# A gated recurrence and a three-way maxout layer on one core: another order of the same pieces

## The chip, the cores and the metric

The kernel runs on one core of a Trainium2 chip. A core has five instruction streams that run side by side and meet by semaphores: TensorE (PE, matrix products, with its weight loads as PEld), VectorE (DVE), ScalarE (ACT), GpSimd (POOL) and SyncE (SP), which here only issues DMAs. ScalarE can issue DMAs too. The metric is the device time of one execution in microseconds (us); lower is better.

## The reference

Four batches of 8 heads, 768 time steps and a head width of 48. For each head a 48x48 state decays row by row and takes in an outer product at every step:

```
state = alpha[:, :, t, :, None] * state + einsum('bhd,bhe->bhde', k[:, :, t], v[:, :, t])
y[:, :, t] = einsum('bhd,bhde->bhe', q[:, :, t], state)
```

The outputs of all heads, side by side (3072 tokens x 384), go through a layer with three weight matrices and a maximum, and an output matrix:

```
h = np.maximum(np.maximum(x @ w1, x @ w2), x @ w3)      # 384 -> 768
out = h @ w_out                                          # 768 -> 384, float32
```

## The kernel before

The 3072 tokens are cut into 12 steps of 256 tokens; steps 0 to 3 are the first 256 tokens of the four batches, 4 to 7 the second, 8 to 11 the third. Within a step the recurrence is done in two chunks of 128 tokens: the cumulated decays are sums of logarithms, a product with a triangular matrix gives them for all tokens, keys and queries are scaled by the exponentials, a masked product of scaled queries and keys gives the part of a chunk within itself, and the state that is carried from chunk to chunk gives the rest.

All work of all steps is cut into pieces, each a small function of step, index and engine. One string, ORDER, lists the pieces; `emit` goes through it from left to right and issues each. `h1v@3` reads: piece h, index 1, on VectorE (v; a is ScalarE, p GpSimd, nothing is the piece's default), step 3. Each engine gets its instructions in the order of the string, and a piece starts when those before it on its engine and what it reads are done. So nothing is planned while the kernel runs: the string is the plan. The pieces:

- `l` loads 256 tokens (384 KB) of alpha, key, query or value (index 0 to 3) into a ring of four buffers, so the load of step s waits for the last reader of step s-4. `K` loads one of 12 parts (384 KB) of the weights into one of 8 staging buffers, `W` casts it to 16 bits (L104 to L111, L174 on). Without a letter, the load is issued by SyncE; with `a`, by ScalarE (L85 to L97).
- `m`, `N`, `r`: products of neighbouring decays, their logarithms, inverses. `u`, `w`: keys and queries of the even tokens scaled by their neighbour's decay. `c`: the sums of the logarithms on TensorE (L207, L209). `e`, `f`, `g`: exponentials of them. `k`, `q`: the scalings of keys and queries (L231). `V`, `v`: scaled values, and their copies by chunk.
- `T`, `t`: turn scaled keys and queries on TensorE, copy them out of PSUM (L265, L151); `D`: turn them by a DMA that SyncE issues (L273). Steps 0 to 4 use `T`, steps 5 to 11 `D`.
- `A`, `a`: scores on TensorE (L286), masks on VectorE (L293). `Y`: outputs on TensorE (L306); even indices are the part within a chunk, odd ones the state's. `x` copies them out as the input x of the layer.
- `M`, `S`, `s`, `z`, `y`: the state: products of gates, update on TensorE (L357), sum (L367), decay (L372), copies in 16 bits.
- `G`: a gate, 6 products of 256 columns (L388), nine for each step; `h`: for every third gate a plain eviction from PSUM (L149 on ScalarE or L151 on VectorE), for the others a maximum on VectorE (L405).
- `O`, `o`: the output projection, 6 products of 384 columns (L421), and its scaling (L155 on ScalarE, L157 on VectorE) with the store that SyncE issues (L430).
- `H`: idle products: so many 128x512 products on a block of zeros, into a PSUM bank that nobody reads (L435).

Everything that TensorE writes goes into eight PSUM banks that are handed out in turn; a piece that needs one waits until the reader of an earlier one is done. Each `H` takes one bank, however many products it has. There are 8 semaphores for DMAs, so a DMA also waits for the eighth before it.

Of the kernel before, what the change touches and what calls it, by code (L numbers as in the profile page):

```python
# [23 lines left out]
def kernel(  # L24
# [422 lines left out]
    def emit(order):  # L447
# [11 lines left out]
        Y3@0 l0@3 v1a@1 t0v@1 m0v@3 A1@1 A0@1 x0a@0 x1a@0 G1@0 K2@0 W2p@0 G2@0 l1@2 a2@1 v0a@1  # L459
        y0p@1 Y3@1 k1p@2 u0p@2 a1@1 N0@3 c0@3 a3@1 a0@1 Y0@1 r0@2 r1@2 K0@0 W0a@0 x0v@1 Y2@1  # L460
        x1a@1 l2@2 s1v@0 s1v@1 f0@3 k0p@2 w0v@2 G0@0 l3@2 M0p@2 G1@1 G0@1 G2@1 h0a@0 q1v@2 T1@2
        g0@3 K5@0 K3@0 e0@3 h1v@0 V0a@2 S0@2 s0a@2 h0v@1 q0p@2 h1v@1 T0@2 t0a@2 t1v@2 W5p@0 G5@1
        G5@0 W3a@0 z0p@2 y0a@2 s1v@2 l0@4 v1p@2 h2v@0 K4@0 h2v@1 r0@4 A1@2 A0@2 a0@2 G3@1 h3a@1
        Y3@2 m0p@4 W4p@0 l3a@3 a3@2 G3@0 N0@4 a1@2 v0p@2 l1@3 r0@3 G4@1 c0@4 g0@4 a2@2 Y2@2
        x1v@2 h3a@0 Y0@2 x0a@2 u0p@3 h4v@1 l0@5 G4@0 h5v@1 M1p@0 z1p@0 y1a@0 G0@2 h0a@2 G5@2
        r1@3 G1@2 K6@0 W6a@0 G3@2 h4v@0 h5v@0 h1v@2 G2@2 l2@3 k0p@3 w0v@3 q0v@3 K7@0 G6@2 V0a@3
        h3a@2 l2@4 l1@4 r1@4 m0p@5 M0p@3 h2v@2 G4@2 h4v@2 k1p@3 S0@3 s0v@3 N0@5 G6@1 h6a@2 h5v@2
        W7p@0 r0@5 G7@2 h7v@2 T0@3 q1p@3 T1@3 G7@1 z0p@3 K8@0 e0@4 w0p@4 f0@4 l3@4 s1v@3 v0a@3
        t1v@3 t0a@3 k1v@4 G6@0 h6a@1 q1p@4 h7v@1 l2@6 u0p@4 c0@5 A0@3 a0@3 A1@3 T1@4 q0p@4 a2@3
        W8a@0 G8@2 a3@3 h8v@2 G8@0 g0@5 h6a@0 a1@3 f0@5 G8@1 k0p@4 T0@4 e0@5 h8v@1 G7@0 v1p@3  # L470
        Y0@3 Y2@3 t1a@4 V0a@4 t0a@4 h7v@0 y0p@3 Y3@3 x0a@3 x1a@3 K11@0 l1@5 K9a@0 v1p@4 S0@4
        W11a@0 A0@4 s0v@4 K10a@0 a1@4 A1@4 a3@4 M0p@4 z0p@4 s1v@4 u0p@5 G0@3 l0@6 a0@4 G7@3
        l1a@6 a2@4 v0v@4 y0a@4 m0p@6 r0@6 G3@3 h3a@3 G1@3 G6@3 Y0@4 r1@5 l3a@5 h0v@3 Y3@4 h8v@0
        Y2@4 x1v@4 N0@6 Y1@4 x0a@4 W9a@0 l2@5 G8@3 M1v@1 c0@6 e0@6 f0@6 G0@4 h1v@3 k0v@5 q1v@5
        G3@4 w0v@5 q0v@5 M0p@5 W10a@0 g0@6 u0v@6 r1@6 G1@4 l0@7 m0v@7 G2@4 k1p@5 D1@5 h0a@4
        z1p@1 k0p@6 O0@1 h1v@4 w0v@6 D0@5 q0p@6 D0@6 k1p@6 q1p@6 O1@1 N0@7 l0@8 h6a@3 l3@6 h2v@4
        l2@7 l1a@7 o1a@1 h7v@3 D1@6 h3v@4 o0a@1 V0a@5 O0@2 o0a@2 O1@2 y1p@1 G7@4 h8v@3 S0@5 A0@5
# [66 lines left out]
```

## Time and profile before

| | us |
|---|---|
| runs | 149.18, 152.22, 148.98 (median 149.18) |
| span of the profiled execution, first to last instruction | 147.1 |
| runs' median over that span | 2.1 |
| TensorE busy | 137.7 |
| VectorE busy | 120.5 |
| ScalarE busy | 100.7 |
| GpSimd busy | 89.7 |
| first sums / first gate / last product's end | 6.18 / 19.22 / 143.2 |

The page gives no time of its own for the profiled execution beside its span; what lies around the span is therefore taken from the runs. Busy times of TensorE are modelled ends of pipelined products, so that the starts of runs of equal instructions say more on their price than the mean of one. DMA issues and waits don't count as busy.

### The profile page before, as it was taken

The page shows a single profiled execution, that of the slowest core. Times are in us where ns is not written, and L with a number is a line of the kernel's source. Part 1 is how long each engine was busy: PE and PEld are TensorE (multiplying, and loading weights), DVE is VectorE, ACT ScalarE, POOL GpSimd, SP SyncE. Part 2 cuts the span into 40 slices and gives each one's busy share as a digit, 9 for nine tenths or more (in the row PEclk, how much of TensorE's full clock was granted, in tenths as well). Part 3 has the DMA queues.
Part 4 walks back from the last instruction along what each step waited for, and adds up shares of the span by engine and source line. Part 5 has one row for each costly group of instructions (what it writes and reads, how often), then busy time and mean ns, then how long its engine had stood idle before and what let it go on. Part 6 is the DMA issues. An engine that isn't in the chain of part 4 may idle for free.

```text
span 147.1 us, 5524 instructions
## 1 busy us (share of the span) xinstructions
PE 137.7 (94%) x2301; PEld 105.4 (72%) x2301; DVE 120.5 (82%) x224; ACT 100.7 (68%) x207; POOL 89.7 (61%) x147
## 2 busy tenths in 40 slices
PE   6996888999999999999999999999899999999990
PEld 2444567888878886788868877688766788878650
DVE  5378989989999999999959998996979989376610
ACT  3669998878999978958699467795375463213170
POOL 8554999899799926997717959738579800000000
PEclk9999999999999999999999999999999999999999
DMA  5999999999999978999999979999987880021163
GB/s 114 321 325 341 326 312 282 322 288 334 328 298 241 286 225 155 202 289 187 303 156 325 327 218 155 237 269 276 288 117 222 91 113 0 4 75 37 53 241 134
DMA packets 73032, 32.43 MB, mean 220 GB/s; under 512 B 65456, under 2 KB 73008, under 8 KB 73008
## 3 DMA queue, kind: packets, MB, share of 16 engines
q1 hardware_dynamic: 63856, 28.06, 75.8%
q10 hardware_dynamic: 9152, 4.03, 10.5%
q8 instruction: 18, 0.29, 0.8%
q14 instruction: 6, 0.05, 0.1%
HBM read 23.69 MB, written 4.72 MB: 193 GB/s over the span
## 4 chain that ended last, share of the span: by engine, by line
PE 38%; DMA 18%; POOL 16%; ACT 9%; SPq 8%; issue 4%; DVE 4%; POOLq 0%; DVEq 0%; ACTq 0%
PE gps L388 21%; DMA rv<-in_v_dram 11%; PE ops L421 10%; SPq L96 7%; POOL qk L231 6%; DMA ws<-in_moe_w_dram 5%; PE yps L306 3%; DMA qkT<-qk 3%; POOL kept L372 2%; POOL ka L198 2%; PE aps L286 2%; POOL st L151 2%; ACT vu L149 1%; POOL wcat L151 1%; POOL vu L151 1%
## 5 line engine op out<-in xcount | busy, mean ns | idle before, releaser
L388 PE MATMUL gps<-xT,wcat 128*128 128x256 f16 x648 | 76.5, 273 | 1.5 <-DVE hT L405 0.6
L388 PEld LDWEIGHTS <-wcat 128*128 128x128 f16 x648 | 61.2, 98 | 11.7 <-issue 1.1
L293 DVE TENSOR_TENSOR lat<-aps,cp 128x512 f16<-128x512 f32 x48 | 30.3, 681 | 0.5 <-PE aps L286 0.3
L405 DVE TENSOR_TENSOR h<-gps,h 128x512 f16<-128x512 f32 x36 | 24.6, 684 | 2.4 <-PE gps L388 1.2
L405 DVE TENSOR_TENSOR hT<-gps,h 128x512 f16<-128x512 f32 x36 | 24.1, 684 | 1.9 <-PE ops L421 1.3
L421 PE MATMUL ops<-wo,hT 128*128 128x384 f16 (+1 forms) x150 | 25.2, 320 | 0.2 <-ACT h L149 0.2
L149 ACT CAST h<-gps 128x512 f16<-128x512 f32 x28 | 16.2, 583 | 9.0 <-PE gps L388 7.0
L421 PEld LDWEIGHTS <-hT 128*128 128x128 f16 x150 | 14.1, 98 | 8.2 <-issue 0.4
L155 ACT ACTIVATE ob<-ops,c 128x384 f32<-128x384 f32 (+1 forms) x23 | 12.2, 567 | 11.4 <-PE ops L421 11.3
L372 POOL TENSOR_TENSOR kept<-full,gm 128x192 f32<-128x192 f32 x18 | 10.3, 573 | 10.5 <-DVE gm L344 5.0
L151 POOL COPY vu<-vt 64x384 f16<-64x384 f16 x24 | 12.2, 509 | 4.7 <-ACT vt L155 2.8
L149 ACT CAST xT<-yps 128x384 f16<-128x384 f32 x17 | 7.8, 490 | 7.3 <-PE yps L306 7.3
L231 POOL TENSOR_TENSOR qk<-ka,ic 128x384 f16<-128x384 f32 x10 | 10.5, 1054 | 3.6 <-ACT h L149 2.6
L149 ACT COPY vu<-vt 64x384 f16<-64x384 f16 x22 | 11.2, 510 | 0.7 <-DVE vt L157 0.3
L435 PE MATMUL wps<-wo 128*128 128x512 f16 x35 | 9.7, 425 | 1.2 <-DVE wo L511 1.2
L155 ACT ACTIVATE vt<-rv,c 128x768 f16<-128x768 f32 x10 | 9.4, 941 | 1.6 <-DMA rv<-in_v_dram 1.5
L231 POOL TENSOR_TENSOR qk<-rq,ac 128x384 f16<-128x384 f32 x8 | 8.3, 1036 | 1.7 <-DMA rq<-in_q_dram 1.7
L286 PE MATMUL aps<-qkT 48*64 48x128 f16 x384 | 7.7, 219 | 1.3 <-DVE qkT L151 0.8
L198 POOL TENSOR_TENSOR ka<-rk,ra 128x384 f32<-128x384 f32 x8 | 8.4, 1044 | 0.2
L306 PE MATMUL yps<-lat,vu 128*32 128x128 f16 x384 | 8.0, 220 | 0.3 <-DVE lat L293 0.2
L231 POOL TENSOR_TENSOR qk<-rk,ic 128x384 f16<-128x384 f32 x6 | 6.2, 1040 | 3.1 <-DMA rk<-in_k_dram 3.0
L192 ACT ACTIVATE ra<-ra 128x384 f32<-128x384 f32 x12 | 6.3, 524 | 2.5 <-DMA ra<-in_alpha_dram 2.4
(58 smaller groups left out, 192.2 us busy)
## 6 DMA issues: line engine op xcount, KB each, us to landing
ra<-in_alpha_dram SPq DMA_DIRECT2D x12, 384.0 KB, 4.9
out_dram<-ob SPq DMA_DIRECT2D x23, 192.0 KB, 2.2
rq<-in_q_dram SPq DMA_DIRECT2D x11, 384.0 KB, 5.9
rv<-in_v_dram SPq DMA_DIRECT2D x9, 384.0 KB, 5.4
ws<-in_moe_w_dram SPq DMA_DIRECT2D x9, 384.0 KB, 5.9
rk<-in_k_dram SPq DMA_DIRECT2D x8, 384.0 KB, 6.1
rk<-in_k_dram ACTq DMA_DIRECT2D x4, 384.0 KB, 5.5
rv<-in_v_dram ACTq DMA_DIRECT2D x3, 384.0 KB, 5.1
```

Source lines behind the costliest of these rows:

```text
L149: nc.scalar.copy(out=dst, in_=src)
L151: engines[eng].tensor_copy(out=dst, in_=src)
L155: nc.scalar.mul(dst, src, col)
L198: engines[eng or "p"].tensor_mul(near_of[s, "k"], raw("k", s, 0), raw("a", s, 1))
L231: engines[eng or "p"].tensor_mul(dst.rearrange("p a b c -> p (a b) c")[:, :, :D], near_of.pop((s, n)) if r == 0 else raw(n, s, r), dec_of[ ...
L286: nc.tensor.matmul(aps[i][r * J:(r + 1) * J, a * U + x, :], qkT[rows, r, 1, p, cols], qkT[rows, :, 0, p, cols], start=True, stop=True)
L293: nc.vector.tensor_mul(lat_of[s, u][:, i], aps_of[s, u][i], pmask.unsqueeze(1).broadcast_to([P, HP, P]))
L306: nc.tensor.matmul(y_of[s, x][C * m:C * (m + 1), f, :], lhs, rhs, start=(s, x, m) not in begun, stop=last[x] and n == len(todo) - 1)
L372: engines[eng or "p"].tensor_mul(kept, full_of.pop((s, x)), gm_of.pop((s, x)).unsqueeze(2).broadcast_to([P, HP, D]))
L388: nc.tensor.matmul(gps[:, j, :], wcat[:, f, g, jj * P:(jj + 1) * P], xT[:, f].rearrange("p u t -> p (u t)"), start=(f == 0), stop=(f == NF ...
L405: nc.vector.tensor_max(h, gps, h_of[s, i - 1])
L421: nc.tensor.matmul(ops_of[s, o], hT_of[s][:, jj, u * P:(u + 1) * P], wo16[:, jj, cols], start=(jj == 0), stop=(jj == NJ - 1))
```

## The change

ORDER is another string. The pieces are the same ones, each as often as before, and the functions are not touched. What differs:

- the place of nearly every piece;
- the engine of some: 8 store scalings, 4 plain evictions, 4 key scalings, 4 gate products and 2 state products move to VectorE, two pieces of the value scaling to GpSimd, and a few single ones either way;
- the issuer of loads: 10 of the 60 were ScalarE's (8 `l` and 2 `K`); all are SyncE's now, and only the two small constants ahead of the string stay ScalarE's;
- the idle products: H12, H4, H1, H1, H4, H10, H1, H2 before, 35 pieces H1 after, 11 of them ahead of the first `c`.

The beginning, the places around the last loads, and the end, cut:

```
-        l0@0 r0@0 H12@0 H4@0 H1@0 m0p@0 N0@0 c0@0 r1@0 l0@1 m0v@1 l2@0 H1@0 r0@1 f0@0 g0@0 H4@0
-        w0p@0 l1@0 u0v@0 q0v@0 N0@1 c0@1 e0@0 l3@0 V0a@0 r1@1 e0@1 f0@1 l0@2 k1v@0 q1v@0 M0p@0
-        l2@1 k0p@0 l1@1 k1p@1 m0v@2 w0v@1 H10@0 g0@1 N0@2 S0@0 s0a@0 T1@0 t1a@0 c0@2 q1v@1 T0@0
-        z0p@0 f0@2 e0@2 g0@2 q0v@1 H1@0 l3@1 V0a@1 t0v@0 A1@0 A0@0 T1@1 H2@0 u0v@1 a2@0 k0p@1
-        S0@1 T0@1 K1@0 v1a@0 v0p@0 a1@0 a3@0 a0@0 Y0@0 W1a@0 Y2@0 t1v@1 y0p@0 s0a@1 M0p@1 z0p@1
...
-        h4v@3 k1v@7 G3@5 h3a@5 G1@5 h1v@5 c0@8 e0@8 g0@7 f0@8 M1p@3 G5@3 h5v@3 G4@5 Y1@6 A1@6
...
-        O4@11 h8v@11 o1a@9 O6@11 o0a@6 o1a@6 o2a@11 O2@11 O3@11 o0a@11 O5@11 o1a@11 O0@10 o0a@10
+        l0@0 m0v@0 l0@1 l2@0 l1@0 m0p@1 l3@0 l2@1 l0@2 N0@0 H1@0 H1@0 H1@0 H1@0 H1@0 H1@0 H1@0 r0@0 H1@0
+        H1@0 H1@0 H1@0 c0@0 H1@0 r0@1 H1@0 H1@0 H1@0 f0@0 r1@0 q1v@0 w0v@0 r1@1 N0@1 e0@0 g0@0 q0v@0 u0v@0
+        k1v@0 H1@0 H1@0 H1@0 H1@0 c0@1 k0v@0 V0v@0 g0@1 f0@1 w0v@1 q1v@1 e0@1 H1@0 H1@0 H1@0 T1@0 H1@0
+        H1@0 S0@0 q0v@1 l1@1 H1@0 T0@0 H1@0 t0v@0 s0v@0 m0p@2 M0p@0 M0v@1 z0p@0 u0v@1 k0v@1 l3@1 t1a@0
+        v1a@0 r0@2 l1@2 K2@0 K0@0 N0@2 r1@2 K1@0 l2@2 l3@2 k1p@1 y0p@0 v0p@0 H1@0 H1@0 H1@0 H1@0 c0@2 A1@0
+        A0@0 T0@1 H1@0 f0@2 s1v@0 a1@0 l0@3 a2@0 a3@0 a0@0 g0@2 V0a@1 t0a@1 S0@1 T1@1 s0a@1 e0@2 W2a@0
...
+        m0p@10 Y0@6 x1a@6 k0v@8 h7v@5 h2v@5 x0a@6 v0a@7 S0@7 s0v@7 A0@7 v0a@8 N0@10 y1a@4 S0@8 A1@7 s0v@8
+        a0@7 G8@5 G5@5 G0@6 a2@7 O1@3 h4v@5 a3@7 o1a@3 G3@6 G1@6 M1v@5 z0v@8 h8v@5 z0p@7 q0p@8 z1p@5 M0p@9
+        q1p@8 y1a@3 y0a@7 h3v@6 a1@7 D0@8 D1@8 l2@11 l3@9 G5@6 G4@6 Y3@7 Y0@7 Y2@7 m0p@11 u0p@9 k1p@9
...
+        G2@6 G7@7 G7@6 c0@11 f0@10 g0@11 f0@11 e0@10 r1@10 y0p@8 w0p@9 q0p@9 V0p@9 k0p@10 k1p@10 v1p@8
...
+        h7v@11 h8v@11 h5v@11 O1@10 o1a@10 o0v@6 O0@10 O4@11 O5@11 O6@11 O2@11 O3@11 o0v@10 o2a@11 o1v@11
+        o0a@11
```

More of the change, by code (lines that the diff above doesn't have):

```diff
@@ L460 @@
[L460 to L477, printed above, removed]
@@ new lines @@
+        Y3@0 H1@0 Y2@0 x1a@0 Y0@0 H1@0 K4@0 z0p@1 x0a@0 K5@0 y0p@1 W1p@0 K3@0 l1@3 t1v@1 k1v@2 u0v@2 W0a@0
+        v0a@1 A0@1 A1@1 a2@1 a0@1 a3@1 H1@0 H1@0 G2@0 G0@0 G1@0 Y3@1 a1@1 Y0@1 v1a@1 V0a@2 s1v@1 w0v@2
+        Y2@1 k0p@2 q1p@2 T1@2 S0@2 x1v@1 x0a@1 h0a@0 G0@1 q0p@2 l0@4 l2@3 s0a@2 h0a@1 T0@2 t0a@2 M0p@2
+        v0p@2 W4p@0 t1v@2 h1v@0 G1@1 G2@1 h2v@0 m0v@3 h1v@1 A1@2 A0@2 N0@3 a2@2 v1a@2 z0p@2 W5p@0 a0@2
+        a1@2 a3@2 c0@3 y0a@2 G4@0 G4@1 G5@0 Y3@2 K6@0 l2@4 l3@3 l1@4 K7@0 e0@3 r0@3 W3p@0 Y2@2 l0@5 Y0@2
@@ new lines @@
+        h2v@1 s1v@2 G3@0 G3@1 k1v@3 x1a@2 r0@4 x0a@2 r1@3 h3v@0 u0p@3 h3v@1 h4v@0 h4v@1 m0p@4 k0p@3 w0p@3
+        r1@4 N0@4 f0@3 G5@1 G0@2 G3@2 c0@4 q1v@3 q0p@3 w0p@4 W6a@0 h3v@2 h5v@0 h5v@1 h0a@2 e0@4 g0@3 G4@2
+        f0@4 T1@3 G1@2 G2@2 T0@3 t1a@3 V0a@3 g0@4 t0a@3 G5@2 G6@0 K10@0 K8@0 l0@6 l3@4 K9@0 K11@0 l1@7
+        l2@5 h1v@2 h4v@2 h2v@2 l0@7 G6@2 S0@3 k1v@4 h5v@2 A0@3 A1@3 h6a@0 W7a@0 s0a@3 G7@0 G7@2 m0v@5 a1@3
+        a0@3 a3@3 q1p@4 u0p@4 M0p@3 v1p@3 M1p@0 q0p@4 N0@5 h6a@2 v0a@3 k0p@4 W8a@0 G6@1 c0@5 T1@4 T0@4
@@ new lines @@
+        h7v@0 a2@3 h7v@2 m0p@6 z0p@3 z1p@0 y0p@3 t1v@4 G8@0 G8@2 W10p@0 r0@5 g0@5 f0@5 N0@6 V0a@4 h8v@0
+        s1v@3 t0v@4 h8v@2 h6a@1 e0@5 G7@1 G8@1 Y2@3 Y0@3 Y3@3 h7v@1 x0a@3 r1@5 x1v@3 S0@4 A1@4 A0@4 s0v@4
+        v0p@4 M1p@1 M0v@4 z1p@1 z0p@4 a2@4 l1@5 a3@4 a0@4 q1v@5 h8v@1 s1v@4 m0v@7 a1@4 u0v@5 v1p@4 u0p@7
+        l1@6 l2@7 l2@6 l3@5 l3@6 l0@9 w0v@5 k0v@5 W9a@0 W11a@0 c0@6 G0@3 G6@3 O0@2 O1@2 O1@1 G4@3 G3@3
+        y1a@0 y0a@4 r0@7 h6a@3 f0@6 e0@6 r1@7 h0a@3 r0@6 g0@6 Y3@4 Y0@4 Y1@4 Y2@4 q0v@5 x0v@4 k1v@5 D0@5
@@ new lines @@
+        D1@5 G7@3 G1@3 M0v@5 l0@8 y1p@1 u0p@6 x1a@4 N0@7 o1a@2 r1@6 h7v@3 o0a@2 k1v@6 w0v@6 h1v@3 G0@4
+        G8@3 c0@7 G1@4 h0v@4 h8v@3 V0a@5 e0@7 o1a@1 O0@1 G2@4 G3@4 G6@4 g0@7 h1v@4 h2v@4 h3v@4 o0a@1 h3a@3
+        f0@7 h4v@3 q0p@6 k0p@6 w0p@7 m0p@9 M0p@6 S0@5 A1@5 A0@5 s0v@5 a3@5 a1@5 a0@5 N0@9 h6a@4 v1a@5
+        v0a@5 M1p@3 q1p@6 M0p@7 z0p@5 G2@3 c0@9 G5@3 O0@0 G7@4 G8@4 y0p@5 M1p@2 m0p@8 h5v@3 a2@5 h2v@3
+        h7v@4 h8v@4 k1v@7 s1v@5 Y2@5 Y3@5 Y1@5 Y0@5 G4@4 D0@6 l1@8 D1@6 g0@9 f0@9 V0a@6 N0@8 x1a@5 x0a@5
@@ new lines @@
+        a2@8 a0@8 D1@9 a1@8 D0@9 a3@8 l3@11 l2@10 G3@7 O0@5 G8@7 G4@7 G2@7 h8v@7 h1v@7 h2v@7 Y0@8 Y3@8
+        Y1@8 Y2@8 o0a@5 v1a@9 h3a@7 x0a@8 x1a@8 g0@10 S0@9 A1@9 A0@9 r0@11 s0v@9 h4v@7 a3@9 a2@9 a1@9 G5@7
+        G3@8 O0@4 G6@8 O1@4 h3v@8 h6a@8 r1@11 V0v@11 z0p@9 w0p@10 y1p@5 q1p@10 o1v@4 h5v@7 q0v@10 q1p@11
+        a0@9 v1p@10 M0p@10 v0p@9 G4@8 h4v@8 G0@8 G7@8 D1@10 D0@10 O0@7 o0a@7 G1@8 G8@8 O1@7 G5@8 y0p@9
+        h7v@8 M1v@6 w0v@11 q0v@11 o0v@4 h8v@8 h0a@8 o1a@7 Y0@9 Y2@9 Y3@9 x1a@9 Y1@9 z1v@6 x0v@9 S0@10
@@ new lines @@
+        A0@10 A1@10 h5v@8 a2@10 G2@8 G7@9 s0v@10 G6@9 a0@10 h1v@8 h6a@9 G3@9 G8@9 G1@9 h2v@8 a3@10 h7v@9
+        u0p@11 M0p@11 k1p@11 h8v@9 G0@9 O1@8 G2@9 y1a@6 h3a@9 v0a@10 v0p@11 z0p@10 k0p@11 y0p@10 a1@10
+        D1@11 O0@8 D0@11 h0v@9 h1v@9 M1v@7 o1v@8 Y2@10 Y1@10 Y0@10 Y3@10 x0a@10 A0@11 h2v@9 x1v@10 S0@11
+        A1@11 O1@6 G0@10 a3@11 a0@11 z1v@7 o0v@8 s0v@11 h0a@10 o1v@6 G6@10 G2@10 G1@10 G4@9 G7@10 h1v@10
+        h4v@9 a2@11 a1@11 G5@9 h5v@9 z0p@11 y0p@11 v1p@11 y1p@7 G8@10 Y1@11 Y0@11 Y2@11 Y3@11 G4@10 G5@10
@@ L507 @@
+        x1a@11 h6a@10 h2v@10 x0v@11 G4@11 G3@10 h3v@10 h4v@10 G0@11 G7@11 h5v@10 G3@11 h3v@11 h7v@10
+        h0a@11 G1@11 O0@9 O1@9 G2@11 o0a@9 O0@6 G6@11 h8v@10 h1v@11 G8@11 G5@11 h6a@11 o1a@9 h2v@11 h4v@11
+        h7v@11 h8v@11 h5v@11 O1@10 o1a@10 o0v@6 O0@10 O4@11 O5@11 O6@11 O2@11 O3@11 o0v@10 o2a@11 o1v@11
+        o0a@11
     """
```

34 lines of the change are left out of this document (6 added, 28 removed).

## The prediction

> **What bounds the kernel now.** I read the page's first part, then the busy times by stretch, the timeline of TensorE and VectorE over the head, the groups, the waits, and the chain that ended last.
>
> ```profile
> span 147.1 us, 5524 instructions
> PE 137.7 (94%) x2301; PEld 105.4 (72%) x2301; DVE 120.5 (82%) x224; ACT 100.7 (68%) x207; POOL 89.7 (61%) x147
> ```
> ```profile
> 30.00:60.00 30.00, 29.74 (x501) 24.43 (x500) 28.35 (x51) 26.84 (x54) 23.96 (x35) 1.00 0.98 269
> 60.00:90.00 30.00, 29.91 (x574) 24.25 (x573) 27.50 (x50) 22.53 (x50) 21.51 (x37) 1.00 1.06 245
> 90.00:120.00 30.00, 29.19 (x509) 22.53 (x507) 26.43 (x47) 18.63 (x39) 20.88 (x35) 1.00 0.98 201
> 120.00:143.20 23.20, 23.05 (x273) 17.63 (x272) 14.51 (x25) 8.49 (x18) 0.51 (x1) 1.00 0.21 73
> ```
>
> The columns of the stretches are PE, PEld, DVE, ACT, POOL busy, then clock, DMA share, GB/s. From 30 us to the last product at 143.2, PE stands for 1.31 us in all, at a granted clock of 1.00. VectorE is next: 28.35 of 30 us, with 1.65 us idle. So the body is held by TensorE with VectorE a little behind; what can still go is the head.
>
> ```profile
> 1.19 5.15 PE L435 MATMUL wps<-wo 128*128 128x512 f16 x17 [1.19 <-DVE wo L511]
> 6.18 0.33 PE L207 MATMUL lps<-la,cp 128*128 128x384 f16 x1
> ...
> 22.52 2.79 PE L388 MATMUL gps<-xT,wcat 128*128 128x256 f16 x24 [0.56 <-ACT wcat L149]
> ...
> 27.93 0.64 PE L286 MATMUL aps<-qkT 48*64 48x128 f16 x32
> ```
> ```profile
> 14.51 2.47 DVE L293 TENSOR_TENSOR lat<-aps,cp 128x512 f16<-128x512 f32 x4
> ...
> 28.71 1.88 DVE L293 TENSOR_TENSOR lat<-aps,cp 128x512 f16<-128x512 f32 x3
> ```
>
> Runs of equal instructions give the price of a piece back to back, without the overlap that a mean of single ones counts twice. PE: a gate of 6 products 0.683 us (24 in 2.73), a projection 0.98, a chunk 0.22, a state part 0.28, scores 0.27, a turn 0.45, an update 0.37, sums 0.26, an idle product 0.23 (ten in 2.32; colder at the start, 17 in 5.15). Over the order: 134.3 us, of which 35 idle products are 8.1. VectorE: 0.62 for a mask or a maximum (four in 2.47), 0.5 for a 128x384 product, 0.57 for a store's scaling, 0.3 for a sum of states: 113.6 us over the order, beside 2.7 of clearing. The page's 120.5 is 1.033 times that, a factor that I keep.
>
> Now PE's time at a place of the order: at the second scores of step 2 (end 28.5) the order holds 21.4 us of PE work, so PE is 7.1 us behind its own sum. 134.3 + 7.1 = 141.4 without another stall; the last product ended at 143.2. All stalls after the head are 1.8 us. Behind it lie 0.58 us for the last scaling and the store, to 147.1. The shown runs are 148.98 and 149.18 at best, about 2.0 us more than the span; I add 2.0.
>
> **The change, part by part.**
>
> *The idle products.* 35 before, 35 after, all ahead of the first gate: no PE work is saved. Eleven instead of 17 precede the first sums. Scaling the 17 (cold for some 3 us, then 0.21 each), eleven end near 5.1. The product of decays that the sums wait for goes to VectorE (0.55 against 1.0 on POOL, both free at 4.4), its logarithm now comes before the inverse's; sums at 5.5 in place of 6.18. But eight idle products follow, and the second sums wait for their own decays: about 7.8, against 7.85 now. Gain there: nothing.
>
> *The head after that.* Loads land one by one, by the waits at 4.4, 5.7, 7.0, 8.2, 9.3, 11.8 (seventh), 13.0 and 14.2, the twelfth at 19.0. The three weight blocks of the first gates are loads 10, 12 and 14 now and 11, 12 and 13 then; the values of step 2 go from 16th to 15th. Following the order engine by engine: the first turn can go at 9.5 instead of 11.0, but VectorE's masks of step 0 still start at 14.8 (14.5 now), because the third sums wait for the third alpha and VectorE has all four scalings of step 0 and its values to itself. First gate 19.6 (weight landed 18.0, its cast, two copies of x, all on ScalarE in a row) against 19.2. Scores of step 2 end at 27.0, sums of step 3 at 27.3, where the order holds 20.1 us of PE work: 7.2 behind, against 7.1. **Head: +0.1**, and I trust it to 1.5 us either way.
>
> *Work between engines.* Counting the engine letters: 8 store scalings go from ScalarE to VectorE (8 x 0.618), 4 plain evictions (4 x 0.685), 4 tiny gate products and 4 key scalings (0.16 and 0.6 each) and 2 state products come to VectorE, two decays, one query and one near product leave: +8.9 us, to 129.4. ScalarE loses some 10 us and ten DMA issues of 0.4; POOL gains 1 to 3: two of its pieces are the scaling of values (128x768), which POOL doesn't do before. Its bounds are the weight cast of that size, 0.82, and two of its 128x384 products, 2.0; I take 1.3, nearer the cast, since it too reads one tensor.
>
> *What this does beside PE.* I sum both engines' pieces up to the n-th gate and set each at its own time: PE at 7.2 (7.1 before) plus its sum; VectorE from where the head leaves it, 30.2 at a sum of 22.3 (30.6 at 21.0 before), times 1.033. Before, VectorE is at 48.5 at gate 30 with PE at 49.1; 53.6 and 54.5 at gate 36; 66.7 and 69.0 at gate 48. After: 54.0 and **52.4** at gate 30, 58.0 and 57.8 at gate 36, 74.1 and **73.2** at gate 48, 98.3 and 98.5 at gate 72, and clear beyond (102.9 and 105.5 at gate 78). VectorE was always ahead by 0.6 us or more; now it is behind by up to 1.6 us over some 45 us. Eight PSUM banks are all that lies between them, so PE waits for evictions: **+1.6**. VectorE's own idle time, free until now (1.65 us between 30 and 60), would come on top; PE's 1.8 us of stalls would partly lie in it. I leave both as they are.
>
> *All loads on SyncE.* Before, 10 of 60 are issued by ScalarE, the first at 29.4. SyncE's queue is in order, and a transpose or a store that waits holds every load behind it: the first two lines are waits of SyncE's queue, the others steps of the chain that ended last.
>
> ```profile
> SPq L430 <- DVE ob L157: 16.9, 2, 10.7
> SPq L273 <- DVE qk L231: 13.0, 4, 8.7
> ```
> ```profile
> 98.32 9.45 DMA rv<-in_v_dram
> 107.80 0.63 DVE vt L157
> ```
>
> Against that stands that most loads come earlier: at gate 48, 56 have been issued in the order, 45 before. In PE time between release and first use the leads after the head are 11 us or more, but for the values of step 8 (7.5), the queries of step 8 (9.4) and the values of step 9 (5.6, 12.3 before). A load lands 5.4 us after its issue (3.7 to 9.4), so the median covers them: 0 in the sum, the long one is a rival. The Trainium skill (DMA: Bandwidth & Descriptors, Issuing engines are not separate DMA queues) says that loads from several engines share the same 16 DMA engines, so a second issuer saves only issue time; by it alone this part is worth nothing either way, and it says nothing of a queue that waits.
>
> *The end.* Last come two products of the last projection, then four stores within 1.2 us of PE work instead of the last one alone; a store of 192 KB lands in 1.7 to 2.1 us and takes 0.5 at 360 GB/s: 0 to 0.5, I take **+0.2**.
>
> Sum: 147.1 + 0.1 + 1.6 + 0.2 = 149.0, and 2.0 around it: **151.0 us**, 1.2% over the median. A change of this kernel under 2% (3 us) can hardly be told from none.
>
> **Rivals.**
>
> *VectorE doesn't bind* (0.25). The 1.033 comes from rows that POOL drew out (0.867 us for some scalings that take 0.548 elsewhere), and the lag over eight banks is small. Then the sum is the head and the end alone: 149.4, and 148 to 149.5 with the head's error.
>
> *The head or the stalls shrink* (0.10). A turn 1.5 us earlier comes through, and the 1.8 us of stalls go: 149.4 - 1.5 - 1.5 = 146.4. Against it: the masks wait for alpha's and the keys' landing in both. The Trainium skill (Trainium Kernel Development and Optimization, Performance Expectations) holds the matmul row to be a poor gauge and weight loads a better one; by the page's 72% there would be more to win than 94% tells. My sum agrees that 8.1 us of PE's work is idle products, but a different order doesn't remove what they wait beside.
>
> *SyncE's queue holds the values of step 9* (0.20): the slower side. They stand behind two transposes that wait for a POOL scaling at 75.3 of PE's sum (82.5 us); issued at 85.5, they land at 90.9 by the median and at 95.0 with the 9.45 of the same load before. POOL scales them itself, and behind that (1.3) stand two key scalings (1.0 each) and the copy of step 8's values (1.05), without which PE's chunk at 89.6 (96.8 us) can't start: ready 95.3 or 99.4, a stall of 0 or 2.6. It decides from a landing over 6.9 us on. With the tie above: 153.6.
>
> The forecast has 0.45. **Range**: 147.3 to 155.0: below, an undisturbed VectorE with the head 1.5 us better; above, the held queue with the head 1.5 us worse. Faster by over 2% only in half of the shrinking head (0.06); slower in the held queue and a third of the forecast (0.35); within 2%, 0.59.
>
> **What would show it.** PE's stretches between 30 and 75 us lose 1.5 to 3 us to evictions and masks, VectorE at 97% or more there; scores of step 2 end near 27.0; from 75 us on PE is as dense as before. It is wrong if PE shows the same 1.3 us of idle time after 30, if the first gates come before 18 or after 21, or if the waits of POOL and ScalarE for values, of 2 us or more, pass to PE.

## The result, and the profile after

| | before | after |
|---|---|---|
| median of the runs, us | 149.31 (148.98 to 152.22) | 154.43 (153.51 to 155.13) |
| ratio | | 1.0335, interval 1.0287 to 1.0384 |
| span of the profiled execution, us | 147.1 | 153.1 |
| mean granted clock over the span | 1.000 | 0.973 |

The changed kernel is 3.4% slower: 5.1 us where 1.8 were forecast. In what follows, ratios leave disturbed executions out, medians and ranges are of all; the profiled executions of four runs (the order before with all loads on SyncE, the run with one load behind the turns, the one with more loads, the one with the turns of steps 5 and 6) are disturbed ones, over 1.5% above the best of their own kernel, so that their places and waits are read and their sums are rough.

The page of the changed kernel, first lines:

```profile
span 153.1 us, 5517 instructions
PE 140.2 (92%) x2301; PEld 106.9 (70%) x2301; DVE 127.4 (83%) x241; ACT 91.1 (59%) x190; POOL 95.0 (62%) x147
```

VectorE is 6.9 us busier, ScalarE 9.6 less, GpSimd 5.3 more: the work moved as the letters of the pieces say. The stretches of the changed kernel, in the columns of the prediction (PE, PEld, DVE, ACT, POOL busy, clock, DMA share, GB/s):

```profile
30.00:60.00 30.00, 28.94 (x483) 23.48 (x472) 28.33 (x52) 25.26 (x53) 22.49 (x32) 1.00 1.05 296
60.00:90.00 30.00, 26.31 (x480) 20.04 (x479) 23.63 (x44) 20.08 (x45) 22.34 (x35) 0.89 1.12 241
90.00:120.00 30.00, 29.34 (x506) 23.73 (x504) 27.13 (x48) 13.80 (x31) 25.18 (x34) 1.00 0.76 172
120.00:149.30 29.30, 29.22 (x379) 23.07 (x376) 23.29 (x41) 7.98 (x16) 4.64 (x11) 1.00 0.25 71
```

Between 60 and 90 us TensorE is busy for 26.31 us where it was busy for 29.91, and 26.31 counts instructions at a clock of 0.89. VectorE falls there too, from 27.50 to 23.63: it isn't what TensorE waits for. The timeline of TensorE in that stretch names the place (start, length, instruction; in brackets how long the engine stood and for what):

```profile
69.83 0.82 PE L388 MATMUL gps<-xT,wcat 128*128 128x256 f16 x6
70.58 0.44 PE L357 MATMUL sps<-vt,qk 64*64 64x48 f16 x32
74.10 1.07 PE L286 MATMUL aps<-qkT 48*64 48x128 f16 x32 [3.09 <-DMA qkT<-qk]
...
75.55 1.44 PE L388 MATMUL gps<-xT,wcat 128*128 128x256 f16 x6
76.78 3.77 PE L421 MATMUL ops<-wo,hT 128*128 128x384 f16 x12
```

The scores of step 6 stand for their turned keys and queries, 3.09 us. Behind that everything takes about double: 12 projection products in 3.77 us where two projections cost 1.96, a gate 1.23 from its start to the next instruction's (75.55 to 76.78) where it costs 0.683. The records have the granted clock at 0.5 from 73.3 to 80.1. From 74.10 to 80.1 at half speed is 3.0 us lost; with the standstill 6.1, and the spans differ by 6.0.

The timeline of SyncE's queue and the chain that ended last say why the turned data is late:

```profile
62.40 2.11 SPq L430 DMA_DIRECT2D out_dram<-ob  x4
64.61 1.46 SPq L273 DMA_TRANSPOSE qkT<-qk  x1
66.13 0.95 SPq L96 DMA_DIRECT2D rk<-in_k_dram  x1
67.20 2.88 SPq L273 DMA_TRANSPOSE qkT<-qk  x1
```
```profile
66.69 0.38 ACT ac L221
67.06 0.13 ACT vt L155
67.20 6.77 DMA qkT<-qk
73.97 0.14 issue
74.10 1.07 PE aps L286 x28
```

The second turn of step 6 is issued at 67.20, behind four stores, the first turn and the keys of step 8, and lands 6.77 us later (a turn's median on the page is 3.6). In the kernel before, the same turn is issued at 65.08 and lands 4.9 us later, at 70.0; the first product that reads it starts at 70.11, the scores behind it, and nothing stands:

```profile
65.08 1.28 SPq L273 DMA_TRANSPOSE qkT<-qk  x1
```
```profile
70.11 0.35 PE L306 MATMUL yps<-qkT,st 128*32 128x128 f16 x12
70.39 0.64 PE L286 MATMUL aps<-qkT 48*64 48x128 f16 x32
```

So the order before had 0.1 us to spare here.

To see where the rest of the time is, I take the prediction's own measure further: the end of the n-th gate's last product minus the sum of the prices of all PE work ahead of it in the order (turns, idle products and all, at the prices of the prediction).

| behind its own sum at gate | 18 | 42 | 48 | 60 | 78 | 108 |
|---|---|---|---|---|---|---|
| before, us | 7.2 | 7.5 | 7.4 | 7.5 | 7.8 | 8.9 |
| after, us | 7.1 | 9.7 | 15.7 | 16.0 | 15.7 | 15.0 |

So the head costs the same (7.1 and 7.2), 2.3 us more are lost between gates 18 and 42, 6.1 at the one place, and behind it the changed order loses 2.2 less than the one before. The head's lines of the changed kernel, to be held against those of before:

```profile
1.17 4.45 PE L435 MATMUL wps<-wo 128*128 128x512 f16 x11 [1.17 <-DVE wo L508]
5.45 0.33 PE L207 MATMUL lps<-la,cp 128*128 128x384 f16 x1
...
7.90 0.32 PE L207 MATMUL lps<-la,cp 128*128 128x384 f16 x1 [0.29 <-ACT la L187]
```
```profile
19.28 2.43 PE L388 MATMUL gps<-xT,wcat 128*128 128x256 f16 x18
...
26.55 0.64 PE L286 MATMUL aps<-qkT 48*64 48x128 f16 x32
27.12 0.34 PE L207 MATMUL lps<-la,cp 128*128 128x384 f16 x1
```
```profile
14.37 2.48 DVE L293 TENSOR_TENSOR lat<-aps,cp 128x512 f16<-128x512 f32 x4
```

Sums at 5.45 and 7.90, VectorE's first masks at 14.37 (14.51 before), the first gate at 19.28, the last scores of step 2 done at 27.1.

### The profile page after: what moved, and what is told of

The parts are those of the page before. It is cut to its first block, busy times and chain, and to the rows that moved or that the text cites. A ratio compares the mean times of both kernels' runs of the same rounds, so it can differ in the third digit from the quotient of the medians.

```text
span 153.1 us, 5517 instructions
## 1 busy us (share of the span) xinstructions
PE 140.2 (92%) x2301; PEld 106.9 (70%) x2301; DVE 127.4 (83%) x241; ACT 91.1 (59%) x190; POOL 95.0 (62%) x147
## 4 chain that ended last, share of the span: by engine, by line
PE 46%; DMA 17%; SPq 10%; DVE 10%; ACT 7%; issue 3%; POOL 3%; DVEq 0%; ACTq 0%; POOLq 0%
PE gps L388 26%; PE ops L421 13%; SPq L96 9%; DMA ws<-in_moe_w_dram 8%; DMA ra<-in_alpha_dram 5%; DMA qkT<-qk 4%; PE yps L306 3%; PE aps L286 2%; POOL qk L231 2%; DVE h L405 2%; DVE hT L405 2%; DVE lat L293 2%; SPq L107 1%; ACT vu L149 1%; DVE qk L231 1%
## 5 line engine op out<-in xcount | busy, mean ns | idle before, releaser
L388 PE MATMUL gps<-xT,wcat 128*128 128x256 f16 x648 | 78.4, 274 | 1.5 <-ACT xT L149 0.7
L421 PE MATMUL ops<-wo,hT 128*128 128x384 f16 (+1 forms) x150 | 27.9, 334 | 0.0
L149 ACT CAST h<-gps 128x512 f16<-128x512 f32 x24 | 14.0, 587 | 19.3 <-PE gps L388 13.9
L155 ACT ACTIVATE ob<-ops,c 128x384 f32<-128x384 f32 (+1 forms) x15 | 8.6, 571 | 10.4 <-PE ops L421 10.4
L183 POOL TENSOR_TENSOR pa<-ra 128x384 f32<-128x384 f32 x8 | 8.7, 1085 | 8.6 <-DMA ra<-in_alpha_dram 8.5
L149 ACT CAST xT<-yps 128x384 f16<-128x384 f32 x17 | 7.7, 477 | 10.2 <-PE yps L306 10.2
L151 POOL CAST st<-kept 64x192 f16<-64x192 f32 x24 | 9.9, 414 | 1.0
L151 DVE CAST h<-gps 128x512 f16<-128x512 f32 x12 | 8.2, 685 | 2.5 <-PE gps L388 2.5
L286 PEld LDWEIGHTS <-qkT 48*64 48x64 f16 x384 | 6.6, 111 | 4.6 <-issue 4.3
L187 ACT ACTIVATE la<-pa 128x384 f16<-128x384 f32 x12 | 6.3, 522 | 5.9 <-DVE pa L183 3.8
L221 ACT ACTIVATE ac<-lps 128x384 f32<-128x384 f32 x12 | 5.9, 488 | 5.9 <-PE lps L209 5.8
```

Of the source, the lines that this page charges most:

```text
L149: nc.scalar.copy(out=dst, in_=src)
L151: engines[eng].tensor_copy(out=dst, in_=src)
L155: nc.scalar.mul(dst, src, col)
L183: engines[eng or "p"].tensor_mul(pair_of[s], raw("a", s, 0), raw("a", s, 1))
L286: nc.tensor.matmul(aps[i][r * J:(r + 1) * J, a * U + x, :], qkT[rows, r, 1, p, cols], qkT[rows, :, 0, p, cols], start=True, stop=True)
L388: nc.tensor.matmul(gps[:, j, :], wcat[:, f, g, jj * P:(jj + 1) * P], xT[:, f].rearrange("p u t -> p (u t)"), start=(f == 0), stop=(f == NF ...
```

## The experiments

The late turn can be late because of where it stands in SyncE's queue (*queue*), because the DMA engines have more to bring than they can by then, whatever the order (*demand*), or because the order of the engines' work costs time that only shows at a DMA (*engines*). The first eight runs move single things; of the later ones one sorts the queue, and the others take DMA work away or add it. The forecasts of the first eight use older names: theory A is the late turn and the half clock behind it, A2 adds that the DMA engines are full and turns stand behind early loads (*queue* and *demand* in one); rival B is one queue for all loads; C is VectorE's added work and D is GpSimd's work, both of them *engines*.

### Idle products ahead of the late scores

```
-        A0@6
+        H14@0 A0@6
```

> Fourteen idle products (3.0 us at full clock) stand between the update and the scores of step 6, where the changed kernel waits 3.1 us for a DMA turn and then runs at half clock for 6.8 us. Theory A (late turn, and the half clock that follows the standstill): the turn lands as late as before, but the clock stays at 1.00, so only the cold part is won, 2.5 to 3 us: about 151.5. Rival C (VectorE's added work makes the loss): PE gets 3 us more work at a place where it is late anyway, no gain, 154 to 155. Rival B (all loads on one queue): nothing changes in the queue, 154 to 155.

154.87 us (153.71 to 155.25), ratio 1.0364 (1.0309 to 1.0418). The clock stays at 1.00 to the end of TensorE's work, so it is the standstill that halves it. No time comes back: the 3.2 us of idle products are added, and later waits appear (1.3 us for a copy of values by GpSimd, 0.9 for another turn). Without the idle products TensorE is 10.4 us behind at gate 48 and 11.6 at gate 108.

### One load behind the turn, then four stores as well, then two turns ahead of three loads

```
-        D0@6 l1@8 D1@6
+        D0@6 D1@6 l1@8
```

> The load of step 8's keys goes behind the second turn of step 6 instead of between the two. Theory A: the second turn is issued about 1 us earlier and shares the DMA engines with one load less, so it lands 1 to 3 us earlier; the standstill shrinks to 0 to 2 us, the clock may hold: 148.5 to 153. Rival C: no change, 154 to 155. Rival B: no change, since the number of loads on the queue is the same.

155.65 us (152.95 to 158.22), no gain that can be told. The turn of step 6 comes in time, and the scores of step 7 stand for 3.04 us at 82.7 for theirs, with the clock at 0.5 from 82.2 to 89.1.

The second run also takes the DMAs of four stores (`o1@2 o0@2 o1@1 o0@1`) from their pieces and issues them behind the turns of step 6:

```
-        D0@6 l1@8 D1@6
+        D0@6 D1@6 P1@2 P0@2 P1@1 P0@1 l1@8
```

> As the run before, and the DMAs of four stores (their scalings stay in place) also go behind the two turns of step 6. Theory A: the first turn goes at about 62.4, the second at 64.3 when its query scaling is done, landing near 68, ahead of PE at 70.95; no standstill, clock 1.00 throughout, span 147 to 147.5, time 149 to 149.5, the time before the change. Rival C: VectorE's work is the same, so no more than the standstill of 3.1 goes and comes back at VectorE: 152 to 154. Rival B: the queue is as long as before, 152 to 154.

155.84 us (154.68 to 158.09), ratio 1.0416 (1.0352 to 1.0479). Again the turn of step 7: 3.31 us at 84.8.

The third run puts the turns of step 7 ahead of three loads as well:

```
-        l0@10 D1@7 l2@8 l1@10 D0@7
+        D1@7 D0@7 l0@10 l2@8 l1@10
```

> The two turns of step 6 stand ahead of four stores and a load, and the two turns of step 7 ahead of three loads (the alpha of step 10, the queries of step 8, the keys of step 10) that nothing needs for 10 us. Theory A2 (the DMA engines are full from the start to 100 us, and turns that stand behind early loads come late; freeing step 6 alone only passed the standstill on to step 7): both standstills go, the clock stays at 1.00, PE keeps the 10 us that it is behind its own work at gate 42: 149 to 150.5. Rival D (GpSimd's 16 us of work between gates 54 and 66 hold everything, whatever the queue does): the standstill moves on to step 8, 153 to 155. Rival C (VectorE): 153 to 155.

155.68 us (153.24 to 156.03). Both turns are in time. Now GpSimd stands 2.36 us for the alpha of step 11, issued at 83.7; ScalarE's logarithm waits for GpSimd's product of it, a copy of x stands behind the logarithm in ScalarE's order, and TensorE stands 2.79 us at 92.2 for that copy. Whatever is taken out of the way, another DMA in the queue is late: TensorE is about 16 to 17 us behind by gate 66 in all three. The medians miss the times that theories A and A2 gave for these runs and for the idle products.

### Loads on ScalarE, in both directions

Ten loads back on ScalarE, the changed order kept:

```
-        l3@3 ... K9@0 ... K10@0 ... l1@6 ... l3@5 ... l1@7 ... l3@8 ... l1@9 ... l1@10 ... l2@11
+        l3a@3 ... K9a@0 ... K10a@0 ... l1a@6 ... l3a@5 ... l1a@7 ... l3a@8 ... l1a@9 ... l1a@10 ... l2a@11
```

> The ten loads that ScalarE issued before the change are ScalarE's again, in the changed order. Rival B (one queue for all loads is at fault): most of the 5 us come back, 149 to 151. Theory A: neither the four stores nor the load of step 8's keys, which stand ahead of the second turn, is among the ten, so the turn lands within 1.5 us of where it lands now: 152.5 to 155, with ten issues of 0.4 us on ScalarE. Rival C: no change.

153.99 us (152.41 to 154.5), ratio 1.0292 (1.0215 to 1.0369): the interval covers the changed kernel's own ratio. Standstills of 2.06 and 2.2 us.

The order before, its ten loads moved to SyncE:

```
-        l3a@3 ... K9a@0 ... K10a@0 ... l1a@6 ... l3a@5 ... l1a@7 ... l3a@8 ... l1a@9 ... l1a@10 ... l2a@11
+        l3@3 ... K9@0 ... K10@0 ... l1@6 ... l3@5 ... l1@7 ... l3@8 ... l1@9 ... l1@10 ... l2@11
```

> The kernel before with its ten ScalarE loads on SyncE, at their places in the order. Theory A2: most of the ten stand between turns that have some slack; those that come ahead of a turn with 1 to 2 us of slack may cost a little: 149 to 151. Rival B (one queue for all loads is at fault): 152 to 155.

160.06 us (158.3 to 161.55), ratio 1.0599 (1.0457 to 1.0742). This one part of the change, done alone, costs 6%. The timeline of TensorE in that run:

```profile
67.77 3.33 PE L388 MATMUL gps<-xT,wcat 128*128 128x256 f16 x29
78.34 0.48 PE L207 MATMUL lps<-la,cp 128*128 128x384 f16 x1 [7.24 <-ACT la L187]
```

and SyncE's queue ahead of it:

```profile
56.97 5.53 SPq L273 DMA_TRANSPOSE qkT<-qk  x3
...
64.82 2.91 SPq L96 DMA_DIRECT2D rk<-in_k_dram  x1
```

The keys of step 7, ScalarE's before, stand behind three turns and three loads now and are issued at 64.8. GpSimd's first scaling of these keys starts at 73.7 and stands ahead of a product of decays in GpSimd's order; ScalarE's logarithm and TensorE's sums wait for that product. An order is made for its queues: the same move costs 6% in one and can't be told from none in the other.

### The engine letters

The run with the turns ahead, and four plain evictions and two copies of x moved from VectorE to ScalarE:

```
-        h3v@0 ... h3v@1 ... h3v@2 ... x1v@3 ... x0v@4 ... h0v@4
+        h3a@0 ... h3a@1 ... h3a@2 ... x1a@3 ... x0a@4 ... h0a@4
```

> As the run before, and six evictions ahead of gate 48 go back from VectorE to ScalarE (3.6 us of VectorE's work). The tie of the prediction: PE's lag between gates 18 and 42, which grew from 7.1 to 9.7 us in the changed kernel, grows only to 8 or 8.5; 1 to 2 us less than the run before. Rival (the lag grows by single waits for loads and weight casts, not by VectorE's work): the lag is 9 to 10 at gate 42, and the time is the run before's within 1 us.

155.72 us (154.93 to 155.99), ratio 1.039 (1.0303 to 1.0477). VectorE loses about 3.5 us of work (four evictions of 0.62, two copies of 0.5), nearly all of it ahead of gate 42; at gate 36 TensorE is 8.7 us behind instead of the 9.0 of the changed kernel. But four other runs, whose engines have the changed order up to there (the idle products, and the three on loads and stores behind the turns) are between 8.3 and 10.0 at that gate, so the 0.3 can't be told from nothing, and this run alone neither shows nor excludes a tie with VectorE. The standstill is 3.52 us at 66.4 now, for the turns of step 5.

### Loads earlier in the order before

```
-        D1@6 ... l1@8 ... l3@7 ... l0@9 l2@8
+        l1@8 l3@7 l0@9 l2@8 D1@6
```

> The kernel before with four loads (keys and queries of step 8, values of step 7, alpha of step 9) moved from behind the second turn of step 6 to ahead of it; all else as before. Theory A2: four loads take 4.8 us of full DMA engines, the turn has some 1.4 us to spare, so PE stands for about 3.4 us at the scores of step 6 and, if the clock halves, loses up to 3 more: 152 to 155.5. Rivals C and D (the loss comes from VectorE's or GpSimd's work in the changed order): no loss here, 149 to 150.

156.79 us (156.6 to 157.23), ratio 1.048 (1.038 to 1.058): four loads that stand some pieces earlier than needed are enough to make the kernel before slower than the changed one. The turn of step 6 is issued at 71.9, and the output that reads it stands for 5.14 us at 76.7. Up to here *queue* and *demand* both explain everything.

### Half of the loads' bytes: the decisive pair

Every load of steps 6 to 10 brings four of eight heads; the other heads keep old data.

```
+        heads = H // 2 if 6 <= s <= 10 else H
...
-            rings[n][s % NQ].rearrange("j h r d -> j h (r d)"),
+            rings[n][s % NQ][:, :heads].rearrange("j h r d -> j h (r d)"),
```

> The changed kernel; the 20 loads of steps 6 to 10 bring only the first four heads (192 KB instead of 384), so the outputs of those steps are not the reference's for the other heads; every other instruction stays. By the engine time of such loads (1.45 us of all 16 DMA engines) 14.5 us of DMA work goes. Theory 'demand' (the DMA engines have no rest until 100 us and the changed order uses its inputs earlier than they can bring them): no wait of TensorE for a DMA above 1.5 us, a granted clock of 1.00 from 30 us on, TensorE at most 10.5 us behind its own sum of work at gates 48 and 60 (15.7 and 16.0 in the changed kernel), 148.5 to 151 us. Rival 'engines' (the loss comes from the order of the engines' work, banks and evictions, and the DMA is only where it shows): 13 or more behind at gate 60, 153 us or more.

147.38 us (146.65 to 148.51), ratio 0.985 (0.9771 to 0.9929). No instruction of any engine is gone and no order changed, and the loss is away, and 2 us more. Which part of that is the order's is told by the same edit in the order before, beside the changed order once more:

> The kernel before with the same half loads: the 20 loads of steps 6 to 10 bring only the first four heads, so the other heads' outputs of those steps are not the reference's. If the order before has DMA time to spare, it gains at most what single waits for DMAs cost it (0.2 us on TensorE directly, 1.8 us for all its stalls): 147.5 to 149.5 us, within 1% of the kernel before. If it is held by the DMA engines as well: below 147.5.

> The changed order with half loads of steps 6 to 10 once more, on the chip of the run beside it; the other heads' outputs of those steps are not the reference's. By its first run 147.4 us (146.7 to 148.5). If the order as such were better or worse than the one before by 1% or more, the two runs would differ by 1.5 us; if all of the change's loss is DMA time, they agree within 1.5 us.

148.29 us (148.08 to 148.76) for the order before, 147.32 (146.72 to 147.72) for the changed one. The stretches from 30 to 90 us, of the order before and then of the changed one:

```profile
30.00:60.00 30.00, 29.23 (x496) 24.09 (x494) 28.03 (x50) 26.03 (x53) 22.60 (x34) 1.00 0.86 235
60.00:90.00 30.00, 29.79 (x572) 24.09 (x570) 27.54 (x49) 22.59 (x49) 21.52 (x37) 1.00 0.71 170
```
```profile
30.00:60.00 30.00, 28.73 (x497) 23.69 (x486) 27.90 (x53) 26.53 (x57) 23.59 (x33) 1.00 0.96 260
60.00:90.00 30.00, 30.00 (x592) 24.22 (x590) 28.14 (x54) 23.74 (x53) 28.70 (x42) 1.00 0.96 210
```

Even with half the bytes the changed order keeps the DMA engines at 0.96, where the order before lets them fall to 0.86 and 0.71: it asks for more in the same time. TensorE from 60 to 90 us is at 30.00 of 30 in the changed order, with no wait for any DMA in the whole run. So with full loads the changed order is 5 us slower, with half loads 1 us faster: *engines* is out, C and D with it, and all of the loss, some 6 us, goes with DMA work. A half load also leaves the queue sooner, so this pair doesn't part *demand* from *queue*. The order before gains 1.3% by its ratio, a little over the 1% that was set for an order with DMA time to spare.

| behind its own sum at gate | 18 | 42 | 48 | 60 | 78 | 108 |
|---|---|---|---|---|---|---|
| before, half loads | 7.3 | 8.3 | 8.1 | 8.4 | 8.8 | 8.9 |
| after, half loads | 7.3 | 8.5 | 8.3 | 8.1 | 7.8 | 7.1 |

### The queue in the order of need

Behind the 27th load, the loads and turns of the changed kernel are sorted by first use, each as early as its buffer allows; 33 of 60 loads and all turns are open to the sort, and no other piece moves. A part of SyncE's sequence, changed kernel and sorted:

```
-  l1@6 l2@7 l2@6 l3@5 l3@6 l0@9 D0@5 D1@5 l0@8 ... D0@6 l1@8 D1@6 l3@8 l3@7 l0@10 D1@7 l2@8 l1@10 D0@7
+  l1@6 l2@6 l3@5 l2@7 l0@9 l0@8 l3@6 l3@8 D0@5 D1@5 ... l1@8 ... D0@6 D1@6 l3@7 l0@10 l2@8 D1@7 ... D0@7
```

> The changed kernel; the loads and turns behind the 27th load are put into SyncE's queue in the order in which their data is first used, as soon as their buffers are free; nothing else moves. Rival 'queue' (the DMA engines could bring all in time, and only the order of the queue is wrong): standstills of 2 us or more gone, 148.5 to 150.5 us. Theory 'demand': by a running sum of DMA work in that order at 1.13 times its engine time, the turns of steps 5 and 6 still come some 7 us later than TensorE's sum of work asks for, as much as TensorE is behind anyway; so part of the 6 us comes back and not all: 11.5 to 14 behind at gate 60, 151.5 to 154 us. Rival 'engines': no change, 154 to 155.

154.1 us (153.24 to 155.07), ratio 1.03 (1.0201 to 1.0398); 14.2 behind at gate 60. The waits of TensorE in that run (total, times, longest):

```profile
PE aps L286 <- DMA qkT<-qk: 4.0, 1, 4.0
```

It is the turns of step 5 now. The time lies just above *demand*'s range and in that of *engines*, which the half loads exclude. This order of the queue, made by a sum that I can follow, gives back nothing that can be told; it doesn't show that no order of the queue could.

### More loads in the order before

Ten loads of 192 KB into buffers that nobody reads, one behind each of ten loads:

```
-        l2@3 k0p@3 w0v@3 q0v@3 K7@0
+        l2@3 B0@0 k0p@3 w0v@3 q0v@3 K7@0 B1@0
```

> The kernel before; ten loads of 192 KB into buffers that nobody reads are added to SyncE's queue, one behind each of ten loads and weight loads between gates 14 and 38; 7.2 us of DMA work by the engine time of such loads. Theory 'demand': the order before is only 3 to 6 us ahead of the DMA there, so TensorE comes to 11 to 14 us behind its sum at gate 48 (7.4 in the kernel before): 153 to 156 us. If the DMA engines had room: 149 to 150.5.

156.65 us (154.78 to 157.45), ratio 1.0421 (1.0311 to 1.0531). Some 7.2 us of DMA work cost the order before 6 to 7 us. TensorE stands 2.85 us at 46.2 for a cast weight and 2.9 us later; it is 15.3 behind at gate 48, where 11 to 14 were expected. The order before has little DMA time to spare between gates 14 and 38 either; the added loads also take places in SyncE's queue and among the 8 semaphores, so this run doesn't part the two causes.

### Turns on TensorE

The six turns of steps 5 to 7, in the places where the DMAs were issued:

```
-        D0@6 l1@8 D1@6
+        T0@6 t0v@6 l1@8 T1@6 t1a@6
```

> The changed kernel; the six DMA turns of steps 5 to 7 are done on TensorE (0.45 us each, 2.7 in all) and copied out by VectorE (three, 0.63) and ScalarE (three, 1.0). 11 us of DMA work goes and no score of these steps waits for a DMA. Theory 'demand': the 6 us of the standstill and the half clock go, 2.7 of TensorE work come: 150 to 152.5 us, at most 12.5 behind at gate 60 with the 2.7 in it. Rival 'engines': 155.5 to 158, since the evictions come on top.

157.81 us (156.16 to 158.46), ratio 1.0523 (1.0425 to 1.0621): a time that *engines* gave, but the profile shows another reason. ScalarE's timeline in that run:

```profile
66.24 2.09 ACT L149 COPY vu<-vt 64x384 f16<-64x384 f16 x4
72.20 1.01 ACT L149 COPY qkT<-tps 128x1024 f16<-128x1024 f16 x1 [3.87 <-PE tps L265]
...
74.89 0.87 ACT L149 CAST xT<-yps 128x384 f16<-128x384 f32 x2
```

ScalarE stands 3.87 us for a turn that TensorE does late, and the copies of x that TensorE needs next stand behind it; TensorE then stands 3.6 us for them and runs at half clock from 75.7 to 79.1. The experiment brought its own stall. So the turns of step 6 alone, and then of steps 5 and 6, were put where no copy of x stands behind them:

```
-        D0@6 l1@8 D1@6 ... x1a@5 x0a@5
+        l1@8 ... x1a@5 x0a@5 T0@6 T1@6 t0v@6 t1a@6
```

> The changed kernel; the two DMA turns of step 6 alone are done on TensorE (0.9 us), ahead of the first gate of step 5, and copied out by VectorE and ScalarE behind the copies of x of step 5, so that no copy of x waits for them. 3.8 us of DMA work goes, and the data that the standstill of 3.1 us waited for no longer comes by DMA. Theory 'demand': the standstill and the half clock behind it go; the arrears of DMA work that are left (5 to 6 us for the alphas of step 7, the keys of step 5 and the values of step 9) are below the 9 us that TensorE is behind: 10 to 12.5 behind at gate 60, 0.9 of it the turns; 149 to 151.5 us. Against it, if any relief only hands the wait on, as in the earlier orders of the queue: another standstill of 2 us or more behind gate 48, 153 to 155.

151.43 us (150.74 to 152.54), ratio 1.0135 (1.0038 to 1.0231): 3 us better than the changed kernel, with 0.9 us more work on TensorE. TensorE is 10.9 behind at gate 60 without the turns, 11.8 with them. Its waits:

```profile
PE yps L306 <- POOL vu L151: 1.2, 1, 1.2
...
PE aps L286 <- DMA qkT<-qk: 1.1, 1, 1.1
```

No standstill over 1.3 us is left, and the clock isn't halved before TensorE's work ends. The wait wasn't handed on this time, as it was by each new order of the queue: here about 3 us of DMA work are gone (125.2 us before the edit, 122.3 after, by the share of the main queue times the span).

For steps 5 and 6 also:

```
-        D0@5 D1@5 ... G8@3 c0@7 G1@4
+        G8@3 c0@7 G1@4 T0@5 T1@5 t0a@5 t1v@5
```

> The same, and the two turns of step 5 on TensorE too, behind the second gate of step 4, copied out by ScalarE and VectorE: 1.8 us of TensorE work for 7.6 us of DMA work. Theory 'demand': no standstill above 1.5 us behind gate 30, 10 to 12 behind at gate 60 with 1.8 of it the turns, 149 to 151 us, so about the kernel before. If TensorE's turns themselves are what cost (banks, copies on engines that are nearly full): 153 or more.

152.94 us (150.87 to 154.71), ratio 1.0205 (1.0085 to 1.0325). Two standstills of 1.10 and 0.78 us for the copies of the turns, 0.6 us apart, and half clock from 64.6 to 68.0 behind them; the profiled execution also ran at half clock from 16.8 to 23.6, in a head in which nothing was changed. Whether more turns on TensorE help stays open. None of the versions beats the kernel before with the whole computation in it.

## Why the prediction was wrong, point by point

**The step that failed** is *All loads on SyncE*, "a load lands 5.4 us after its issue (3.7 to 9.4), so the median covers them: 0 in the sum". It took a landing time as a property of a load and set each load's own lead against it, one by one. The pair of half loads shows the order losing some 6 us to DMAs, which this step costs at nothing. DMA time is a stock that all share: the page's third part gives the share of the queues' packets, 86.3% of 147.1 us before (127 us of the 16 engines) and 82.2% of 153.1 after (126 us), the same work; and the changed kernel's DMA share is 1.05 from 30 to 60 us and 1.12 from 60 to 90. (The share is a sum of packet times; as it goes over 1, packets overlap, and 1 is no sharp limit.) The right question was how much must have been brought by when. By TensorE's sum of work, the changed order has used 38 loads at 40 us and the one before 32; at 48 both have used 38; at 62, about where the scores of step 6 stand, 45 and 44; at 70, 50 and 44; at 78, 55 and 49. So it asks for up to six loads sooner, 8.8 us of DMA work at 1.46 us each (worked out below), but not at every place; this count, an estimate from the strings alone, gives a direction and not the size or the place of the loss. The row for it was there: a DMA share of 0.98 to 1.06 in all stretches up to 120 us.

The same step counted the leads of loads only. The six turns of steps 5 to 7 are DMAs in the same queue, their lead is short (scaled keys to scores), and they are what was late in most of the runs. The prediction saw turns as something that holds loads up, never as something that loads hold up.

What stays open is how much of the 6 us comes from the amount of DMA work asked for by then and how much from its order in SyncE's queue. For the order: ten loads moved to SyncE cost the order before 6% with the same DMA work. For the amount: the sorted queue gave nothing back, and two turns less gave 3 us back.

*By the Trainium skill* (DMA: Bandwidth & Descriptors, Issuing engines are not separate DMA queues) a second issuer saves only issue time. Ten loads moved from ScalarE to SyncE cost the order before 6%: there the rule misses what stands in the queue ahead of them. In the changed order, moving them back can't be told from nothing, as the rule has it.

*The head*: right. Sums at 5.45 (5.5), second sums at 7.90 (7.8), first gate at 19.28 (19.6), scores of step 2 done at 27.1 (27.0), 7.1 behind (7.2).

*What this does beside PE, +1.6*: right in place and size by chance (2.3 lost between gates 18 and 42), wrong in its cause. VectorE is busy for 28.33 of 30 us from 30 to 60, not 97%; TensorE's waits there are single ones of 0.18 to 0.33 us, two for a cast weight, one for a mask, one for a state, 1.0 us in all (what makes the rest of the 2.3 is open); and with half loads, VectorE's work unchanged, the two orders are 8.3 and 8.5 behind at gate 42. A tie of the engines' sums did not bind by 1.6 us over eight banks, as the first rival said.

*VectorE's sum*: 129.4 forecast, 127.4 on the page. *GpSimd's value scaling*: 2.21 us, twice, where 1.3 was taken and 2.0 was the upper bound; the bound came from other forms and didn't hold. It cost nothing that shows.

*The end, +0.2*: 0. From the last product to the end of the span it is 3.9 us in both (143.2 to 147.1, 149.2 to 153.1).

*The stalls, left as they are*: between gates 48 and 108 the order before falls 1.5 us further behind and the changed one gains 0.7. That is 2.2 us for the changed order, not forecast; with half loads it is 2.0, and the order is faster for it.

*The rivals.* The held values of step 9 had the right kind of mechanism, DMAs held in one queue, and with 153.6 nearly the right time, but the wrong place: GpSimd stood 0.89 us for those values, and no chunk waited for it. The victim was the turn of step 6, 20 us earlier. Its price had no half clock in it, which is half of the loss. The shrinking head didn't come (half of its 0.10 is 0.05, where the prediction has 0.06).

So the range held the time, for a reason that isn't in it.

## What to carry to other kernels

Where the DMA share of the stretches is near 1.0, a new order has to be checked as a budget: cumulated DMA work by first use, turns and stores with the loads, against time, and each turn's place behind the loads with it; a landing time from the old order says nothing on the new one. When one wait is taken away and another of the same length appears further on, look for the shared stock behind both, and take some of its work away (half the bytes) to prove it, with the same edit in the old order beside it. Price a standstill of TensorE of 3 us or more with the half clock behind it: about 1.6 to 3.2 us again here.

## What the runs showed of the hardware

**Half clock.** All eight standstills of TensorE of 3.04 to 7.24 us went with a granted clock of 0.5, for 3.4 us (after 3.31, 3.64, 3.97 and 5.14), 6.8 (3.04, 3.09, 3.52) or 10.2 (7.24). Of five between 2.06 and 2.92 us three did (2.06, 2.79, 2.85) and two didn't (2.17, 2.92). Single ones of up to 1.3 did nothing, but in the run with the turns of steps 5 and 6 two groups of short ones were enough: 1.10 and 0.78 us with 0.6 us of turns between them were followed by 3.4 us of half clock, and in its head 1.36 us at 14.4 and 1.11 at 17.2 went with 6.8 us of it from 16.8. So the stretches come in steps of 3.4 us, and between 2 and 3 us a standstill may or may not bring one. The steps agree with the Trainium skill (TensorE: Matmul & The Clock Gate, Part 1: The HAM clock gate), which has a free-running window of about 3.4 us. What the same page gives as the abstract rule, no gaps over 3.4 us, is too kind for this kernel: six gaps of 2.06 to 3.31 us were already enough.

**DMA work of a turn.** From the share of the main queue times the span: 125.2 us in the changed kernel, 110.6 with 20 loads halved, 113.7 with six turns fewer, 118.2 with four fewer, 122.3 with two fewer. That is 1.46 us of all 16 engines for a load of 384 KB and, by these differences, 1.45 (two fewer) to 1.9 (six) for a turn of 256 KB. The trace's packets of 256 bytes, which are the turns' alone, say it directly: 24.8 us for 14 turns in the changed kernel, 1.77 each, and 1.98 each in the kernel before; the packets of 384 bytes of the 48 loads of inputs give 1.50 and 1.45 a load. By the byte that is 1.8 to 2 times as much for a turn. The Trainium skill (Advanced Engine Details and Errata, X-Bar Transpose (TRN2)) calls transposing DMAs as fast as regular ones; by engine time per byte the runs of this case disagree.
